# An embedding norm moved to GpSimd, a reordered start of the attention, a state kept in compact form, and one note per gated step

## The chip, the cores and the metric

The program runs on one core of one Trainium2 chip. The metric is the device time of one execution in microseconds. Engines are called by the names of the profile: PE is TensorE (PEld its weight loads), DVE is VectorE, ACT is ScalarE, POOL is GpSimd, SP is the engine whose queue issues the loads.

## The reference

Three stages follow each other; all is float32.

```python
# 1. gated linear attention, B,H,S,D = 4,8,768,40
m_new = np.maximum(f_gate[:, :, t] + m, i_gate[:, :, t])
f_stab = np.exp(f_gate[:, :, t] + m - m_new)
i_stab = np.exp(i_gate[:, :, t] - m_new)
C = f_stab[:, :, None, None] * C + i_stab[:, :, None, None] * np.einsum('bhd,bhe->bhde', vt, kt)
n = f_stab[:, :, None] * n + i_stab[:, :, None] * kt
h_tilde = np.einsum('bhde,bhe->bhd', C, qt)
denom = np.maximum(np.abs(np.einsum('bhd,bhd->bh', n, qt)[:, :, None]), 1.0)
y[:, :, t] = o * h_tilde / denom                      # o = sigmoid(o_gate)
# 2. mixture of 8 experts on the 3072 rows of 320, one expert a row
en = expert_emb / (np.linalg.norm(expert_emb, axis=-1, keepdims=True) + 1e-06)
logits = xn @ en.T / tau                              # xn: rows normed alike
expert_idx = np.argmax(logits, axis=1)
h = np.maximum(x[mask] @ w1[e], 0.0)                  # F = 1024
out[mask] = gate_w[mask, None] * (h @ w2[e])
# 3. gated unit, F = 1536
gate = 1.0 / (1.0 + np.exp(-(x @ w_gate)))
val = x @ w_val
out = (gate * val) @ w_out
```

## The kernel before

**Attention.** The 768 steps are cut into 6 chunks c of 128; with 4 batches b that makes 24 tiles, i = 4c + b. A tile goes through hand-written steps. `st_S` multiplies keys and queries of the 8 heads on PE into two PSUM banks; DVE masks each bank (`am`, and the second in place), ACT casts both to f16 (`ah`), and the remainders `al` are subtracted, the first half on POOL, the second on DVE. `st_V` weights the values on POOL (`vw`), `st_V2` splits them into `vh` (ACT) and `vl` (POOL). `st_AV` multiplies: for c > 0 first the queries with the state `cst[b]` (L464), then the three products of `ah`, `al` with `vh`, `vl` (L471 to L473). `st_U` multiplies keys and weighted values into bank 5 (`u_ps`, L484), and its `add` brings that into the state: for chunk 0 two ACT copies (L493), afterwards two DVE operations (L495). Even heads lie on partitions 0 to 39, odd ones on 64 to 103, hence two of each. `post_ops` divides by the denominator on DVE (`den`, `x0`) and multiplies with the gate on POOL; `st_XT` transposes the result on PE, ACT copies it (`xt`), and `st_logit` multiplies with the transposed, normed embedding `enT`; DVE copies the result to `rs`. `warm(n)` are n matmuls without use.

Each engine runs its instructions in the order in which the code issues them. In the main loop over i, PE's order is the state product and AV of tile i, XT of i-1, U of i, S of i+3, the logits of i-1. Tiles 0 to 3 and the S of tiles 1 to 5 stand ahead of the loop, written out.

**Gates.** `gate_ops` are six DVE operations on 32 rows (two scans, four sums); they run for chunk 0, for chunk 1, and once for chunks 2 to 5 (512 wide). `st_gexp` takes exponentials on ACT, `st_gates2` transposes them on PE (for chunks 2 to 5 into bank 5) and copies them on DVE to `w_all` and `ri_all`. `sideq` is a list of such small operations, and `side(n)` issues n of them wherever it stands. The square root of the embedding norm is a seed and three Newton steps of three operations, on 8 x 1 elements (`sqrt_ops`), on DVE, through `sideq`.

**Experts** follow, then the **gated unit** in 72 steps t. `gated_a(t)` and `gated_b(t)` make gate and value in two PSUM banks out of a ring of four; each bank is written first from one half of the rows and then from the other, and between the two halves PE waits for a tiny ACT copy, `note`, that waits for the first (`turn_rows`). Then follow a sigmoid on ACT, a product on DVE (both `sgm`), a cast on ACT (`hh`), a remainder on POOL (`hl`) and the second product, `gated_l2h(t - 2)`, on PE. Steps 0 and 1 begin together: both `gated_a`, then both `gated_b`. `group_x` splits the input of a later group with an ACT cast (L209) and a POOL subtraction.

Of the kernel before, what the change touches and what calls it, by code (L numbers as in the profile page):

```python
# [22 lines left out]
def kernel(  # L23
# [250 lines left out]
    def kpart(i):  # L274
        return kv[i % NKV][:, KO:VO].rearrange("p (h d) -> p h d", d=D)
# [28 lines left out]
    def emb_norm():  # L304
        esq = ap_.tile([NE, DM], F32, name="esq")
        en1 = ap_.tile([NE, 4], F32, name="en1")
        return [
            lambda: nc.scalar.activation(out=esq, in_=eb, func=AF.Square, accum_out=en1[:, 0:1])
        ] + sqrt_ops(ap_, en1[:, 1:2], en1[:, 0:1]) + [
            lambda: nc.vector.tensor_scalar(  # L310
                out=en1[:, 2:3], in0=en1[:, 1:2], scalar1=1e-6, scalar2=tb, op0=ALU.add, op1=ALU.mult
            ),
            lambda: nc.vector.reciprocal(en1[:, 3:4], en1[:, 2:3]),
            lambda: nc.vector.tensor_scalar_mul(eb, eb, en1[:, 3:4]),
        ]
# [15 lines left out]
    for j in range(4):  # L331
        if j:
            load_qk(j)
        load_kv(j)
        if j == 1:
            nc.sync.dma_start(out=eb, in_=emb)
            nc.sync.dma_start(out=tb, in_=tau.rearrange("(a b) -> a b", a=1).to_broadcast([NE, 1]))
# [55 lines left out]
    def emb_T():  # L393
# [6 lines left out]
        nc.vector.tensor_copy(enT[:, 0:2].rearrange("p a b -> p (a b)"), tp[:, 0:2 * NE])  # L400
        nc.vector.tensor_copy(enT[0:RM, 2], tp[0:RM, 2 * NE:3 * NE])
# [74 lines left out]
    def st_U(i):  # L476
# [92 lines left out]
    def st_rank(c):  # L569
# [14 lines left out]
        pf = bp.tile([P, B, NE], F32, tag="pf", name="pf")  # L584
# [116 lines left out]

    for op in gate_ops(0, L):
        op()
    st_gexp(0, L)
    st_S(0, lambda: st_gates2(0, 1))
# [6 lines left out]
    def early(i):  # L712

        st_AV(i)
        post[i] = post_ops(i)
        weave(post[i][0:3] + post[i][4:5], [side] * 4)


    sideq += gate_ops(L, 2 * L)
    st_V(0)  # L720
    side(6)
    st_V2(0)
    sideq += emb_norm()
    side(1)
    act_zero(qk[0])
    st_gexp(L, 2 * L)
    st_S(1)
    st_V(1)
    st_V(2)
    st_S(2, lambda: (early(0), st_V2(1)))  # L730
# [9 lines left out]
    st_S(3, lambda: early(1))  # L740
    st_U(1)
    st_V2(3)
    side(2)
    post[1][5]()
    load(5)
    st_S(4, lambda: (st_XT(0), early(2), side(len(sideq))))
    st_sig(2)
    load_kv(6)
    post[2][5]()
    st_V(4)  # L750
    st_U(2)
    st_S(5, lambda: (st_XT(1), emb_T(), st_AV(3), st_post(3)))
    sideq += gate_ops(2 * L, S)
    GX = 5
    for i in range(3, NTILE - B):
        load(i + 4)
        if i > 3:
# [3 lines left out]
            st_V2(i + 1)  # L761
            post = post_ops(i)
# [3 lines left out]
        else:  # L766
            warm(5)
# [27 lines left out]
        def between():  # L795
            if add:
                add()
            st_logit(i - 1)

        then = (lambda: st_logit(1)) if i == 3 else first_rows if i == NTILE - B - 1 else None  # L800
        st_S(i + NAHEAD, then, between)
# [8 lines left out]
        if i == GX:  # L810
            st_sig(GX + 1)
            st_gexp(2 * L, S)
# [787 lines left out]
    def gated_a(t):  # L1600
# [6 lines left out]
        note(ins[-1], "l1")  # L1607

    def gated_b(t):
        g, f = order2[t]  # L1610
        fs = slice(f * P, (f + 1) * P)
        for kk in range(2):
# [4 lines left out]
            if kk == 0 and "l1" in passed:  # L1617
# [509 lines left out]
```

## Time and profile before

| | us |
|---|---|
| median of 3 runs (lowest, highest) | 763.08 (761.12, 763.3) |
| profiled execution, its own time | 759.18 |
| its span, first to last instruction | 757.4 |
| PE busy in the span | 727.0 |
| DVE, ACT, POOL busy | 403.3, 364.5, 397.4 |
| mean granted clock of PE, share of full | 0.993 |

The profiled execution is 3.9 us shorter than the median of the timed ones. The 1.8 us between its time and its span lie outside the instructions.

### The profile page before, as it was taken

Reading aid. Unit: us, or ns where it says so; the run is one execution under the profiler, and the core shown is the slowest. Engines: PE = TensorE matmul, PEld = TensorE weight load, DVE = VectorE, ACT = ScalarE, POOL = GpSimd, SP = SyncE. Lnnn points to the kernel's source line nnn. Section 1 sums busy time; section 2 is a strip of 40 time slices with the busy share of each in tenths; the row PEclk is TensorE's granted clock in tenths of the full one; section 3 lists DMA queues with packets and bytes.
Section 4 is the critical chain, followed back from the end, with each engine's and each line's share of the span. In section 5 each row is a group of like instructions: output and inputs, shape, how many; then the busy total and the mean of one; then the engine's idle time right before and its main releaser. Section 6 shows DMA issues by size and latency. Waiting matters only on the chain. (4 is left out here: it accounts for less than half of the span.)

```text
span 757.4 us, 17682 instructions
## 1 busy us (share of the span) xinstructions
PE 727.0 (96%) x6906; PEld 645.3 (85%) x6906; DVE 403.3 (53%) x864; ACT 364.5 (48%) x829; POOL 397.4 (52%) x449
## 2 busy tenths in 40 slices
PE   6889999899999999999899999999999999999995
PEld 5779998799888989999688888888888888888884
DVE  7897999877778777865566664132121111111111
ACT  5765664645965656665454444333333333333322
POOL 6767887757766777886053233542324324324222
PEclk9999999999999999999999999999999999999999
DMA  7654875545455556651112210000000000000001
GB/s 221 193 160 122 265 217 162 168 119 163 146 153 160 157 158 193 185 150 53 53 57 81 81 54 19 37 35 2 1 12 27 2 1 37 1 2 35 2 1 39
DMA packets 39864, 70.46 MB, mean 93 GB/s; under 512 B 4818, under 2 KB 28460, under 8 KB 39772
## 3 DMA queue, kind: packets, MB, share of 16 engines
q1 hardware_dynamic: 36764, 59.61, 26.7%
q0 software_dynamic: 3008, 9.64, 3.9%
q8 instruction: 56, 0.92, 0.5%
q14 instruction: 36, 0.29, 0.1%
HBM read 60.55 MB, written 8.68 MB: 91 GB/s over the span
## 5 line engine op out<-in xcount | busy, mean ns | idle before, releaser
L1634 POOL TENSOR_TENSOR hl<-sgm,hh 128x512 fp32r<-128x512 f32 x71 | 95.1, 1342 | 228.5 <-ACT hh L1633 228.4
L1623 DVE TENSOR_TENSOR sgm<-v_ps,sgm 128x512 f32<-128x512 f32 (+1 forms) x73 | 49.8, 683 | 231.8 <-ACT sgm L1622 231.8
L1659 PE MATMUL o_ps<-wo,hl 64*128 64x320 f32 x560 | 87.2, 307 | 0.0
L1658 PE MATMUL o_ps<-wo,hh 64*128 64x320 f32 x560 | 86.7, 305 | 0.0
L1657 PE MATMUL o_ps<-wo,hh 64*128 64x320 f32 x560 | 86.4, 304 | 0.0
L1622 ACT ACTIVATE sgm<-g_ps 128x512 f32<-128x512 f32 (+1 forms) x73 | 43.2, 593 | 81.7 <-PE g_ps L1581 74.3
L1593 ACT COPY seen<-zeros 1x1 f32<-1x1 f32 x142 | 27.0, 190 | 105.5 <-PE v_ps L1581 57.6
L1633 ACT CAST hh<-sgm 128x512 fp32r<-128x512 f32 (+1 forms) x73 | 44.8, 615 | 48.1 <-DVE sgm L1623 47.7
L1041 ACT ACTIVATE hh<-h_ps 128x256 fp32r<-128x256 f32 (+7 forms) x72 | 35.3, 490 | 55.1 <-PE h_ps L953 50.1
L1579 PE MATMUL v_ps<-xg,wvh 64*128 64x512 f32 x144 | 56.6, 393 | 2.4 <-ACT seen L1593 2.4
L1657 PEld LDWEIGHTS o_ps<-wo,hh 64*128 64x128 f32 x560 | 53.0, 185 | 6.6 <-issue 0.3
L1658 PEld LDWEIGHTS o_ps<-wo,hh 64*128 64x128 f32 x560 | 52.8, 184 | 5.8
L1579 PE MATMUL g_ps<-xg,wgh 64*128 64x512 f32 x144 | 56.6, 393 | 0.0
L1579 PE MATMUL v_ps<-xh,wvh 64*128 64x512 f32 x144 | 56.5, 392 | 0.0
L1579 PE MATMUL g_ps<-xh,wgh 64*128 64x512 f32 x144 | 56.5, 392 | 0.0
L1580 PE MATMUL g_ps<-xg,wgh 64*128 64x512 f32 x144 | 56.4, 392 | 0.0
L1580 PE MATMUL v_ps<-xl,wvh 64*128 64x512 f32 x144 | 56.4, 392 | 0.0
L1580 PE MATMUL v_ps<-xg,wvh 64*128 64x512 f32 x144 | 56.4, 392 | 0.0
L1580 PE MATMUL g_ps<-xl,wgh 64*128 64x512 f32 x144 | 56.4, 392 | 0.0
L1581 PE MATMUL g_ps<-xg,wgl 64*128 64x512 f32 x144 | 56.2, 390 | 0.0
L1581 PE MATMUL v_ps<-xg,wvl 64*128 64x512 f32 x144 | 56.2, 390 | 0.0
L1581 PE MATMUL v_ps<-xh,wvl 64*128 64x512 f32 x144 | 56.2, 390 | 0.0
(354 smaller groups left out, 2603.8 us busy)
## 6 DMA issues: line engine op xcount, KB each, us to landing
kv<-in_kvo_dram SPq DMA_DIRECT2D x24, 484.0 KB
w2raw<-in_moe_w_dram SPq DMA_DIRECT2D x32, 320.0 KB
w1raw<-in_moe_w_dram SPq DMA_DIRECT2D x32, 256.0 KB
qk<-in_qkt_dram SPq DMA_DIRECT2D x48, 160.0 KB
xs<-x SPq DMA_DIRECT2D x24, 192.0 KB
w1raw<-in_moe_w_dram SPq DMA_DIRECT2D x64, 64.0 KB
raw<-in_moe_w_out_dram SPq DMA_DIRECT2D x12, 320.0 KB
raw<-in_moe_w_gate_dram SPq DMA_DIRECT2D x8, 384.0 KB
```

The lines of the kernel that those rows point to most:

```text
L1041: nc.scalar.activation(out=h[f][0], in_=ps, func=AF.Relu)
L1579: lambda: nc.tensor.matmul(ps, at(wh), h[rows, kk], start=start, stop=False),
L1580: lambda: nc.tensor.matmul(ps, at(wh), l[rows, kk], start=False, stop=False),
L1581: lambda: nc.tensor.matmul(ps, at(wl), h[rows, kk], start=False, stop=stop),
L1593: passed[key] = nc.scalar.copy(seen, zeros[0:1, 0:1])
L1622: nc.scalar.activation(out=s[:, cs], in_=pg[:, cs], func=AF.Sigmoid)
L1623: nc.vector.tensor_tensor(out=s[:, cs], in0=pv[:, cs], in1=s[:, cs], op=ALU.mult)
L1633: nc.scalar.copy(gh[:, cs], s[:, cs])
L1634: e.tensor_tensor(out=gl[:, cs], in0=s[:, cs], in1=gh[:, cs], op=ALU.subtract)
L1657: lambda: nc.tensor.matmul(o, gh[rows, ts_], wh[rows], start=begin, stop=False),
L1658: lambda: nc.tensor.matmul(o, gh[rows, ts_], wl[rows], start=False, stop=False),
L1659: lambda: nc.tensor.matmul(o, gl[rows, ts_], wh[rows], start=False, stop=end),
```

## The change

Five things change together. (1) The norm of the embedding: DVE keeps the two operations of the seed and a reciprocal; the three Newton steps and what follows are 11 operations on POOL, right behind the first `st_V`; the scaling of the embedding is one ACT operation; its load stands three loads earlier. (2) In the first tiles `post_ops` and the copies of `st_gates2` come behind the masks instead of ahead of them (argument `last` of `st_S` in the place of `then`), `warm(2)` stands behind AV of tiles 1, 2 and 3, and three of the five behind tile 3 stay; the gates of chunks 2 to 5 begin one to two tiles earlier. (3) `cc[b]`, 128 x 4 x 41, holds the state without the split by heads: from chunk 2 on one DVE operation on 104 partitions adds to it, in chunk 1 two; two ACT copies spread it to `cst[b]`. So that partitions 40 to 63 of the bank hold numbers, the even heads' matmuls in `st_U` take 64 columns of keys instead of 40. POOL clears the four `cc` at the start. (4) `note` has a key for each step t, where before step 1 overwrote that of step 0, which then waited for step 1 while step 1 waited for nothing. (5) An ACT sigmoid on one column stands ahead of step 0, and `group_x` for group 1 moves from the steps 1, 2, 3 to 2, 3, 4.

```diff
+    cc = [bp.tile([P, NPR, DV], F32, name=f"cc{b}", bufs=1) for b in range(B)]
+    for t in cc:
+        nc.gpsimd.memset(t, 0.0)
...
+    def norm_seed():
+        yi = en_y.bitcast(I32)
+        nc.vector.tensor_single_scalar(out=yi, in_=en_sq.bitcast(I32), scalar=1, op=ALU.logical_shift_right)
...
+    def norm_steps():
+        g = nc.gpsimd
+        two = lambda o, x, u, w, op0, op1: g.tensor_scalar(out=o, in0=x, scalar1=u, scalar2=w, op0=op0, op1=op1)
+        for _ in range(3):
+            two(en_t, en_y, en_sq, en_y, ALU.mult, ALU.mult)
+            two(en_t, en_t, -0.5, 1.5, ALU.mult, ALU.add)
+            g.tensor_tensor(out=en_y, in0=en_t, in1=en_y, op=ALU.mult)
+        g.tensor_tensor(out=en_y, in0=en_y, in1=en_sq, op=ALU.mult)
+        two(en_t, en_y, 1e-6, tb, ALU.add, ALU.mult)
+
+    def norm_scale():
+        nc.vector.reciprocal(en_r, en_t)
+        nc.scalar.activation(out=eb, in_=eb, func=AF.Copy, scale=en_r)
...
         for h in range(H):
             u, pr_ = h % 2, h // 2
+            n = D if u else DP
             nc.tensor.matmul(
-                pu[DP * u:DP * u + D, pr_ * DV:(pr_ + 1) * DV], kpart(i)[:, h], vw[:, h], start=True, stop=True
+                pu[DP * u:DP * u + n, pr_ * DV:(pr_ + 1) * DV], kv[i % NKV][:, h * D:h * D + n], vw[:, h],
+                start=True, stop=True,
             )
 
         def add():
-            for u in range(2):
-                sl = slice(DP * u, DP * u + D)
-                pv = pu[sl, 0:NPR * DV].rearrange("p (a d) -> p a d", a=NPR)
-                if c == 0:
-                    nc.scalar.activation(out=cst[b][sl, :, u], in_=pv, func=AF.Copy, scale=SQ)
-                    continue
+            pv = pu[:, 0:NPR * DV].rearrange("p (a d) -> p a d", a=NPR)
+            both = [slice(DP * u, DP * u + D) for u in range(2)]
+            if c == 0:
+                for u, sl in enumerate(both):
+                    nc.scalar.activation(out=cst[b][sl, :, u], in_=pv[sl], func=AF.Copy, scale=SQ)
+                return
+            before = [(sl, cst[b][sl, :, u]) for u, sl in enumerate(both)]
+            if c > 1:
+                before = [(slice(0, DP + D), cc[b][0:DP + D])]
+            for sl, old in before:
                 nc.vector.scalar_tensor_tensor(
-                    out=cst[b][sl, :, u], in0=pv, scalar=SQ, in1=cst[b][sl, :, u], op0=ALU.mult, op1=ALU.add
+                    out=cc[b][sl], in0=pv[sl], scalar=SQ, in1=old, op0=ALU.mult, op1=ALU.add
                 )
+            for u, sl in enumerate(both):
+                nc.scalar.copy(cst[b][sl, :, u], cc[b][sl])
...
-    st_S(0, lambda: st_gates2(0, 1))
+    st_S(0, None, lambda: (st_gates2(0, 1), norm_seed()))
...
-    sideq += gate_ops(L, 2 * L)
     st_V(0)
-    side(6)
+    norm_steps()
+    weave(gate_ops(L, 2 * L))
...
-    st_S(2, lambda: (early(0), st_V2(1)))
+    st_S(2, lambda: (st_AV(0), st_V2(1)), lambda: first_post(0))
...
-    st_S(3, lambda: early(1))
+    st_S(3, lambda: (st_AV(1), warm(2)), lambda: first_post(1))
...
+    sideq += gate_ops(2 * L, S)
+    side(1)
...
-    GX = 5
+    GX = 4
...
-        note(ins[-1], "l1")
+        note(ins[-1], t)
...
-            if kk == 0 and "l1" in passed:
-                turn_rows(ins[0], "l1")
+            if kk == 0:
+                turn_rows(ins[0], t)
...
-    xsteps = {1 + u: (1, u) for u in range(3)}
+    xsteps = {2 + u: (1, u) for u in range(3)}
...
         if t == 0:
+            nc.scalar.activation(out=dum, in_=zeros[:, 0:1], func=AF.Sigmoid)
             gated_a(0)
```

What moves is seen in the order of the instructions. The first place is DVE at tiles 0 and 1 (`sq_y`, `sq_t` and `en` belong to the norm, `den` and `x` to the denominators). Before:

```order
L455 TENSOR_TENSOR al<-s_ps,ah 128x512
L389 TENSOR_SCALAR w_all<-tp_r 128x32
L389 TENSOR_SCALAR ri_all<-tp_r 128x32
L524 TENSOR_TENSOR den<-o_ps,ri_all 128x8
L163 SCALAR_TENSOR_TENSOR sq_y<-sq_t,sq_y 8x1
L527 SCALAR_TENSOR_TENSOR den<-o_ps,den 128x8
L161 TENSOR_TENSOR sq_t<-sq_y,en_258 8x1
L530 RECIPROCAL den<-den 128x8
L162 SCALAR_TENSOR_TENSOR sq_t<-sq_t,sq_y 8x1
L532 TENSOR_TENSOR x_414<-o_ps,den 128x320
L163 SCALAR_TENSOR_TENSOR sq_y<-sq_t,sq_y 8x1
L447 TENSOR_TENSOR am<-s_ps,cmask 128x512
```

Now the same tile has its masks first, and no operation of the norm:

```order
L403 TENSOR_SCALAR w_all<-tp_r 128x32
L403 TENSOR_SCALAR ri_all<-tp_r 128x32
L463 TENSOR_TENSOR am<-s_ps,cmask 128x512
L465 TENSOR_TENSOR s_ps<-s_ps,cmask 128x512
L548 TENSOR_TENSOR den<-o_ps,ri_all 128x8
L551 SCALAR_TENSOR_TENSOR den<-o_ps,den 128x8
L554 RECIPROCAL den<-den 128x8
L556 TENSOR_TENSOR x_442<-o_ps,den 128x320
L471 TENSOR_TENSOR al<-s_ps,ah 128x512
```

The norm's steps stand on POOL now, between the weighted values of tile 0 and their remainder `vl`, which stood next to each other before:

```order
L425 TENSOR_TENSOR vw<-kv_128,w_all 128x328
L318 TENSOR_SCALAR en_158<-en_158 8x1 x2
L322 TENSOR_TENSOR en_158<-en_158 8x1
L318 TENSOR_SCALAR en_158<-en_158 8x1 x2
L322 TENSOR_TENSOR en_158<-en_158 8x1
L318 TENSOR_SCALAR en_158<-en_158 8x1 x2
L322 TENSOR_TENSOR en_158<-en_158 8x1
L323 TENSOR_TENSOR en_158<-en_158 8x1
L318 TENSOR_SCALAR en_158<-en_158,tb 8x1
L435 TENSOR_TENSOR vl<-vw,vh 128x328
```

The second place is DVE around the masks of tiles 5 and 6, where the 512 wide operations of the gates (`mt`, `ft`, `Gt`) and the copies of the logits (`rs`) lie. Before:

```order
L455 TENSOR_TENSOR al<-s_ps,ah 128x512
L559 COPY rs<-l_ps 128x8
L359 SCALAR_TENSOR_TENSOR mt<-ft,mt,it 32x512
L363 TENSOR_TENSOR ft<-ft,mt 32x512
L559 COPY rs<-l_ps 128x8
L447 TENSOR_TENSOR am<-s_ps,cmask 128x512
```

Now one of the wide operations stands ahead of the first copy, and the gates are further on:

```order
L471 TENSOR_TENSOR al<-s_ps,ah 128x512
L371 TENSOR_TENSOR ft<-ft,mt 32x512
L583 COPY rs<-l_ps 128x8
L379 SCALAR_TENSOR_TENSOR Gt<-ft,Gt,lim 32x512
L371 TENSOR_TENSOR it<-it,mt 32x512
L463 TENSOR_TENSOR am<-s_ps,cmask 128x512
```

The third place is ACT at steps 0 to 2 of the gated unit (`seen` is a note, `wo` a cast of the last weights). Before:

```order
L1593 COPY seen<-zeros 1x1 x2
L1112 ACTIVATE fa<-fa,relu_b 128x320
L1095 CAST wo<-fb 128x320
L1622 ACT_TABLE_LOAD
L1622 ACTIVATE sgm<-g_ps 128x512
L1633 CAST hh<-sgm 128x512
L1112 ACTIVATE fa<-fa,relu_b 128x320
L1622 ACTIVATE sgm<-g_ps 128x512
L1095 CAST wo<-fb 128x320
L1633 CAST hh<-sgm 128x512
L209 CAST xh<-yT 128x512
L1593 COPY seen<-zeros 1x1 x2
```

Now the table load stands ahead of the notes, and the cast for group 1 is no longer ahead of step 2's notes:

```order
L1752 ACT_TABLE_LOAD
L1752 ACTIVATE dum<-zeros 128x1
L1624 COPY seen<-zeros 1x1 x2
L1143 ACTIVATE fa<-fa,relu_b 128x320
L1126 CAST wo<-fb 128x320
L1653 ACTIVATE sgm<-g_ps 128x512
L1664 CAST hh<-sgm 128x512
L1143 ACTIVATE fa<-fa,relu_b 128x320
L1653 ACTIVATE sgm<-g_ps 128x512
L1126 CAST wo<-fb 128x320
L1664 CAST hh<-sgm 128x512
L1624 COPY seen<-zeros 1x1 x2
```

## Rows read from the trace of the kernel before

**Rows 1.** Windows: busy by engine (PE, PEld, DVE, ACT, POOL), granted clock, DMA.

```profile
16.00:31.00 15.00, 11.50 (x141) 10.35 (x139) 12.47 (x39) 9.49 (x21) 10.52 (x14) 0.89 0.55 157
...
45.00:62.00 17.00, 13.72 (x184) 11.78 (x184) 13.87 (x41) 9.41 (x21) 10.89 (x17) 0.90 0.56 171
62.00:120.00 58.00, 57.06 (x895) 53.24 (x894) 52.90 (x152) 36.27 (x85) 47.12 (x73) 1.00 0.67 202
```

**Rows 2.** Waits of PE from 0 to 62 us: total us, times, longest.

```profile
PE u_ps L484 <- ACT cst L493: 2.1, 2, 1.2
...
PE tp_x L543 <- DVE rs L559: 1.4, 1, 1.4
```

**Rows 3.** Windows, columns as in rows 1: the first stretch at half clock.

```profile
26.70:30.10 3.40, 3.40 (x30) 3.32 (x25) 3.34 (x12) 1.53 (x5) 1.86 (x3) 0.50 0.50 139
```

**Rows 4.** Timeline of PE: start us, us, line, operation, count.

```profile
14.81 0.18 PE L471 MATMUL o_ps<-vh,ah 128*128 128x41 f16 x1
...
21.30 2.05 PE L435 MATMUL s_ps<-qk 128*128 128x128 f32 x16
...
27.06 3.48 PE L435 MATMUL s_ps<-qk 128*128 128x128 f32 x16
...
31.67 1.24 PE L426 MATMUL warm_ps<-ones_bf 128*128 128x512 bf16 x5
...
42.09 0.73 PE L555 MATMUL l_ps<-enT,xt 128*128 128x8 f32 x6
42.68 1.10 PE L464 MATMUL o_ps<-cst,qk 128*128 128x82 f32 x8
...
44.85 0.63 PE L543 MATMUL tp_x<-ident,x 128*128 128x128 f32 x3
...
57.40 2.00 PE L464 MATMUL o_ps<-cst,qk 128*128 128x82 f32 x8
...
60.85 0.49 PE L543 MATMUL tp_x<-ident,x 128*128 128x128 f32 x3
```

**Rows 5.** Timeline of DVE, columns as in rows 4.

```profile
21.40 0.79 DVE L161 TENSOR_TENSOR sq_t<-sq_y,en 8x1 f32<-8x1 f32 x1
...
36.90 1.11 DVE L363 TENSOR_TENSOR ft<-ft,mt 32x512 f32<-32x512 f32 x1
...
54.81 0.69 DVE L447 TENSOR_TENSOR am<-s_ps,cmask 128x512 f32<-128x512 f32 x1
...
56.02 0.66 DVE L495 SCALAR_TENSOR_TENSOR cst<-u_ps,cst 40x164 f32<-40x164 f32 x2
```

**Rows 6.** Timeline of POOL, columns as in rows 4.

```profile
12.58 0.81 POOL L419 TENSOR_TENSOR vl<-vw,vh 128x328 f16<-128x328 f32 x1 [0.57 <-ACT vh L418]
...
52.95 1.04 POOL L583 TENSOR_TENSOR run<-run,sel 128x8 bf16<-128x8 bf16 x4
```

**Rows 7.** Groups by form: count, busy us, mean ns; L493 from 0, others from 62, to 120 us.

```profile
L493 ACT ACTIVATE cst<-u_ps 40x164 f32<-40x164 f32 x8 | 2.4, 302 | 0.0
...
L464 PEld LDWEIGHTS o_ps<-cst,qk 128*128 128x128 f32 x96 | 11.7, 192 | 0.0
...
L495 DVE SCALAR_TENSOR_TENSOR cst<-u_ps,cst 40x164 f32<-40x164 f32 x24 | 7.7, 320 | 0.2
...
L484 PEld LDWEIGHTS u_ps<-vw,kv 128*40 128x40 f32 x192 | 4.7, 118 | 2.5 <-PE tp_x L543 2.4
```

**Rows 8.** Timelines of ACT and PE at steps 0 to 2 of the gated unit.

```profile
371.18 1.28 ACT L1622 ACT_TABLE_LOAD   x1
...
378.35 0.61 ACT L209 CAST xh<-yT 128x512 fp32r<-128x512 f32 x1
378.87 0.41 ACT L1593 COPY seen<-zeros 1x1 f32<-1x1 f32 x2
...
379.11 0.50 PE L1579 MATMUL v_ps<-xg,wvh 64*128 64x512 f32 x1 [2.01 <-ACT seen L1593]
```

**Rows 9.** Waits of PE from 100 to 160 us, columns as in rows 2.

```profile
PE s_ps L435 <- DVE am L447: 0.8, 1, 0.8
```

More of the change, by code (lines that the diff above doesn't have):

```diff
@@ L302 @@
     nc.scalar.activation(out=dum, in_=zero, func=AF.Exp)
[L304 to L315, printed above, removed]
+    esq = ap_.tile([NE, DM], F32, name="esq")
+    en1 = ap_.tile([NE, 4], F32, name="en1")
+    en_sq, en_y, en_t, en_r = (en1[:, j:j + 1] for j in range(4))
+    def norm_seed():
+        yi = en_y.bitcast(I32)
+        nc.vector.tensor_single_scalar(out=yi, in_=en_sq.bitcast(I32), scalar=1, op=ALU.logical_shift_right)
+        nc.vector.tensor_scalar(
+            out=yi, in0=yi, scalar1=-1.0, scalar2=float(0x5F3759DF), op0=ALU.mult, op1=ALU.add
+        )
+    def norm_steps():
[10 more added lines that the diff above has]
+        nc.scalar.activation(out=eb, in_=eb, func=AF.Copy, scale=en_r)
     nc.gpsimd.memset(qk[1], 0.0)
@@ L333 @@
             load_qk(j)
+        if j == 0:
+            nc.sync.dma_start(out=eb, in_=emb)
         load_kv(j)
         if j == 1:
-            nc.sync.dma_start(out=eb, in_=emb)
             nc.sync.dma_start(out=tb, in_=tau.rearrange("(a b) -> a b", a=1).to_broadcast([NE, 1]))
@@ L700, in side @@
                 sideq.pop(0)()
+    nc.scalar.activation(out=esq, in_=eb, func=AF.Square, accum_out=en_sq)
     for op in gate_ops(0, L):
@@ L710, with first_post @@
     post = {}
-    def early(i):
-        st_AV(i)
+    def first_post(i):
         post[i] = post_ops(i)
-        weave(post[i][0:3] + post[i][4:5], [side] * 4)
-    sideq += gate_ops(L, 2 * L)
+        weave(post[i][0:3] + post[i][4:5])
     st_V(0)
-    side(6)
+    norm_steps()
+    weave(gate_ops(L, 2 * L))
     st_V2(0)
-    sideq += emb_norm()
-    side(1)
     act_zero(qk[0])
     st_gexp(L, 2 * L)
-    st_S(1)
+    st_S(1, None, norm_scale)
     st_V(1)
     st_V(2)
-    st_S(2, lambda: (early(0), st_V2(1)))
+    st_S(2, lambda: (st_AV(0), st_V2(1)), lambda: first_post(0))
     load(4)
@@ L739 @@
     post[0][5]()
-    st_S(3, lambda: early(1))
+    st_S(3, lambda: (st_AV(1), warm(2)), lambda: first_post(1))
     st_U(1)
     st_V2(3)
-    side(2)
     post[1][5]()
     load(5)
-    st_S(4, lambda: (st_XT(0), early(2), side(len(sideq))))
+    sideq += gate_ops(2 * L, S)
+    side(1)
+    turned = []
+    st_S(
+        4, lambda: (turned.extend(emb_T()), st_XT(0), st_AV(2), warm(2)),
+        lambda: (weave(turned), first_post(2)),
+    )
     st_sig(2)
@@ L749 @@
     post[2][5]()
+    side(1)
     st_V(4)
     st_U(2)
-    st_S(5, lambda: (st_XT(1), emb_T(), st_AV(3), st_post(3)))
-    sideq += gate_ops(2 * L, S)
-    GX = 5
+    st_S(5, lambda: (st_XT(1), st_AV(3), warm(2)), lambda: st_post(3))
+    side(1)
+    GX = 4
     for i in range(3, NTILE - B):
@@ L797, in between @@
                 add()
+            if i == 3:
+                st_logit(1)
             st_logit(i - 1)
-        then = (lambda: st_logit(1)) if i == 3 else first_rows if i == NTILE - B - 1 else None
-        st_S(i + NAHEAD, then, between)
+        st_S(i + NAHEAD, first_rows if i == NTILE - B - 1 else None, between)
         if i > B and i % B == 1:
```

15 lines of the change are left out of this document (8 added, 7 removed).

## The prediction

> **What bounds the kernel now.** I began with PE's busy time by stretches, because a faster DVE, ACT or POOL pays only where PE stands still for it. From 62 to 120 us PE is busy 57.06 of 58.00 us at the full clock [rows 1]: a tile there costs what PE needs, and time freed on DVE (52.90) or ACT (36.27) buys nothing. Two stretches ahead of it are different. PE is idle for 3.50 us of 16 to 31 and for 3.28 us of 45 to 62, and their mean granted clock is 0.89 and 0.90 [rows 1]. Together 6.8 us idle.
>
> The view of PE's waits names the releasers: 2.1 us for ACT to empty the bank of `u_ps` into the state, 1.4 us for a DVE copy of logits [rows 2]. Both queue behind something else. ACT's copies stand behind its casts, which wait for DVE's masks, and the masks stand behind the norm's operations on 8 numbers, one of which took 0.79 us [rows 5]. So the reader should see a queue, not a slow instruction.
>
> After each of the two idle stretches PE runs at half clock, 1.2 instead of 2.4 GHz, for about 3.4 us; the first is granted 0.50 over 3.40 us [rows 3]. The price is read from equal work. S with 16 matmuls took 3.48 us there and 2.05 us at the full clock: 1.4 us. From the start of the state product to the transposes it was 60.85 - 57.40 = 3.45 us in the second and 44.85 - 42.68 = 2.17 us otherwise: 1.3 us [rows 4]. What the first tiles lose is therefore 6.8 + 2.7 = 9.5 us.
>
> Much later, at step 2 of the gated unit, PE waits 2.01 us for a note [rows 8].
>
> **The change, part by part.** The sum is made on the profiled execution of 759.18 us, which is 3.9 us under the median of the runs; I carry the difference over to the median, 763.08.
>
> *First tiles.* With the norm off DVE and the masks ahead of the denominators, the chain mask, cast, state copy runs earlier, and the waits of 16 to 62 us lose their cause; nothing in the rows gives a reason for the half clock to come back without them. That is a gain of up to 9.5 us. Four things are paid out of it.
>
> Four matmuls without use are new: five took 1.24 us [rows 4], so 1.0 us. They fill waits, but I count them, since I have already counted the waits as gone.
>
> A new wait stands at tile 5's logits. DVE's copy of tile 0's logits, which frees the bank that PE takes next, now stands behind a 512 wide gate operation; such a one took 1.11 us [rows 5]. PE, behind it, holds the logits and state product of the next tile. Between 0 and 1.1 us, I take 1.0, because DVE is the late one of the two here.
>
> A second one: the transposes of the gates of chunks 2 to 5 need bank 5, which the state add of the tile before still reads, and now come directly after S. The masks begin at 54.81 and the adds end at 56.02 + 0.66 = 56.68 [rows 5], 1.9 us; only the logits' matmuls of 0.73 us [rows 4] cover that. I take 1.1 us, between 0 and 1.9.
>
> On POOL the norm's 11 steps stand between `vw` and `vl` of tile 0. Four dependent operations on 8 columns took 1.04 us [rows 6], so 11 take 2.9 us. POOL was free from 12.58 - 0.57 = 12.0 us on [rows 6]; `vl` would then end at 12.0 + 2.9 + 0.8 = 15.7 us, where AV of tile 0 began at 14.81 [rows 4]: 0.9 us late at most, less as far as tile 0's masks, now ahead of the copies of the gates, start POOL earlier. I take 0.4. No row shows such a step beside DVE's gate operations. The nearest is the reverse, DVE's operation of 8 numbers that took 0.79 us [rows 5]; at that length eleven would take 8.7 us and AV would be 6.7 us late. The Trainium skill, SBUF — State Buffer, section "SBUF: two separate sides", says that DVE and GpSimd hold their shared ports for a whole instruction, and that a DVE operation with two SBUF inputs is enough to block the other. By that rule steps on POOL are held as that row was, and the sum would be short of up to 6.3 us more; the trace shows the blocking on DVE's side only.
>
> The first tiles then give 9.5 - 1.0 - 1.0 - 1.1 - 0.4 = 6.0 us.
>
> *State.* ACT gets two copies of 0.30 us [rows 7] in each of the 16 tiles 4 to 19, 9.7 us in all. I cost them at nothing: in the 12 tiles of 62 to 120 us ACT is idle for 21.7 us [rows 1], 1.8 us a tile, and the state they write is needed four tiles on. DVE loses one of two adds of 0.32 us [rows 7] in 12 tiles, 3.8 us, and gains in PE's time only where PE waits for DVE's masks, 0.8 us once near the end of the attention [rows 9]; I take 0.4, between 0 and 0.8. The four clears on POOL are half the size of an operation of 0.81 us [rows 6], so up to 1.6 us; I cost them at nothing, as the loads at the start are the cover, and keep that bound.
>
> The matmuls of `st_U` load 64 columns in place of 40 for four heads. A load of 40 took 118 ns, one of 128 took 192 ns [rows 7]: 0.84 ns a column, 20 ns for 24. Each head is two instructions, so 8 loads a tile, 0.16 us. Where PE is the bound, in 16 tiles, that is 2.6 us; in all 20 tiles 3.2 us, and nothing if the loads lie behind matmuls. I take 2.6: the loads follow one another through the whole of `st_U`, which has little else to hide them. Against it the Trainium skill, TensorEngine Tiling (Array Packing), section "Key Properties", says that different tiles of the array load weights and multiply in parallel; even and odd heads are different tiles, and by that rule a longer load could lie beside the other half's matmuls, with a sum of 0 for this term. No row here has 64 columns.
>
> *Gated unit.* The table load of 1.28 us no longer stands ahead of step 0's sigmoid [rows 8], and everything down to step 2's note follows it: the product, the cast, the remainder. The cast for group 1 starts 378.87 - 378.35 = 0.52 us ahead of the note [rows 8] and moves behind it. The note comes 1.8 us earlier, out of a wait of 2.01 us. Between 0.5 (the cast alone) and 2.0; I take 1.8. What group 1 needs of its cast comes four steps later.
>
> Sum: 6.0 + 0.4 - 2.6 + 1.8 = 5.6 us. The profiled execution would take 759.2 - 5.6 = 753.6 us, the median **757.5 us**.
>
> **The rivals.**
> *POOL's steps hold AV of tile 0.* At half way between 0.26 and 0.79 us, 0.53 us each, they take 5.8 us; `vl` ends at 18.6 us and AV is 3.8 us late, 3.4 more than taken: 760.9 us. For it is the row of 0.79 us; against it, that DVE has only six gate operations there, so that not every step can meet one. It decides the verdict from 3.3 us on.
>
> *The loads of `st_U` are hidden.* Then 2.6 us come back: 754.9 us. For it speaks that even and odd heads alternate; against it that PE's loads are busy 53.24 of 58.00 us [rows 1]. This is what the rule on tiles would make of it.
>
> *Slower: ACT's copies stand on the path.* They lie between the casts and the copy `xt` for which PE's logits wait. If all 9.7 us were exposed the time would be 757.5 + 9.7 = 767.2 us. It takes over 5.6 of the 9.7 us, 58%, to turn the sign; ACT's 1.8 us of idle time a tile speak against it.
>
> *The change does not do what it says at the gated unit.* A note per step alone shortens nothing that step 2 waits for, since its note was its own already. If the table load was hidden before and only the cast counts, 1.3 us of the gain go: 758.8 us.
>
> **How the numbers follow.** Chances: my sum 0.45, with a range of its own of 755.5 to 759.5 (one of its new waits more or less); POOL's steps 0.20; hidden loads 0.20; the gated unit without its gain 0.08; slower 0.07. A measurement of this kernel can tell some 0.3%, 2.3 us, from no change, so faster begins under 760.8 us. Faster: all of the sum, of the hidden loads and of the gated case, and half of POOL's case, 0.83; the same 0.11; slower 0.06. For the range, the early end is the hidden loads with both new waits gone as well, 754.9 - 2.1 = 752.8; the late end is POOL's case, 760.9, and a little of its upper bound: 752.8 to 761.3.
>
> **What would show it.** No half-clock stretch once AV of tile 0 has begun; the transposes that stood at 60.85 us [rows 4] about 6 us earlier; a wait of about 1 us ahead of tile 0's or 1's logits, and one of about as much ahead of the transposes of the gates of chunks 2 to 5; AV of tile 0 within half a microsecond of 14.8; `st_U` longer by 0.16 us a tile, and tiles in the steady stretch longer by as much; step 2's wait for its note cut to a fraction. I would be wrong if a half-clock stretch came back (1.3 to 1.4 us each), if DVE's wide gate operations held more than these two waits, or if the steady tiles grew by more than `st_U` does, which would be ACT.

## The result, and the profile after

The changed kernel takes 753.6 us, the median of 4 runs (752.28 to 755.48); the kernel before took 762.1 us in the runs beside it. The ratio is 0.989 (95% interval 0.986 to 0.991): 8.5 us faster, inside the range, and 2.9 us more than the sum of 5.6 us; 753.6 us lies outside the sum's own range of 755.5 to 759.5. The profiled execution took 752.99 us, 6.2 us under that of before. The two totals for the profiled executions are close, but the stages below show that this is in part luck; the other 2.3 us of the gain lie in what the first profile did not show. Two executions among the later runs, 1197.85 us of no_gated and 4005.5 us of the kernel before, belong to a slow state and stand in no median below.

The windows of the changed kernel, columns as in rows 1, the last one a stretch that before ran at the full clock:

```profile
16.00:31.00 15.00, 14.61 (x220) 12.40 (x219) 12.24 (x31) 11.12 (x27) 14.02 (x18) 1.00 0.59 187
45.00:62.00 17.00, 15.79 (x237) 14.36 (x237) 13.20 (x38) 12.79 (x28) 11.79 (x19) 1.00 0.54 175
62.00:120.00 58.00, 57.56 (x867) 53.67 (x864) 49.59 (x143) 40.99 (x104) 46.44 (x74) 1.00 0.65 202
142.90:149.70 6.80, 6.80 (x36) 6.71 (x37) 5.38 (x16) 0.41 (x2) 3.06 (x6) 0.50 0.55 152
```

PE was idle for 6.8 us in the first two [rows 1]; now it is idle for 0.39 and 1.21 us, at the full clock. From 62 to 120 us DVE is busy 3.3 us less and ACT 4.7 us more, and PE is a little fuller than before (57.56 us, 57.06 before). A half-clock stretch has appeared at the end of the attention.

PE's waits from 0 to 62 us (total us, times, longest), to be held against rows 2:

```profile
PE s_ps L451 <- DMA qk<-in_qkt_dram: 4.2, 2, 3.7
PE tp_r L401 <- ACT it L392: 2.1, 1, 2.1
PE tp_r L401 <- DVE cc L517: 1.2, 1, 1.2
PE o_ps L488 <- POOL vl L435: 1.0, 1, 1.0
PE tp_x L567 <- DVE rs L583: 0.2, 1, 0.2
```

The waits of `st_U` for ACT are gone, and that of the transposes for `rs` fell from 1.4 to 0.2 us. The third row is the gates of chunks 2 to 5, which before waited 0.4 us:

```profile
PE tp_r L387 <- DVE cst L495: 0.4, 1, 0.4
```

The fourth row is new at tile 0; the prediction had named both. Behind the fourth stand the norm's steps. POOL's timeline at tile 0 (start us, us, line, operation, count):

```profile
10.64 0.74 POOL L425 TENSOR_TENSOR vw<-kv,w_all 128x328 f32<-128x328 f32 x1
11.36 0.71 POOL L318 TENSOR_SCALAR en<-en 8x1 f32<-8x1 f32 x2
...
12.45 0.93 POOL L318 TENSOR_SCALAR en<-en 8x1 f32<-8x1 f32 x2
...
14.98 0.26 POOL L318 TENSOR_SCALAR en<-en,tb 8x1 f32<-8x1 f32 x1
15.31 0.80 POOL L435 TENSOR_TENSOR vl<-vw,vh 128x328 f16<-128x328 f32 x1
```

Eleven steps from 11.36 to 15.24 us are 3.9 us, 0.35 each. AV of tile 0 began at 14.96 and stood still for `vl` until 16.17:

```profile
16.17 0.18 PE L488 MATMUL o_ps<-vl,ah 128*128 128x41 f16 x1 [1.02 <-POOL vl L435]
```

This wait is not a constant of the kernel. In the eight profiles with the steps on POOL ahead of `vl` it is 0 (early_only, no_warm, best4) or 0.6 to 1.4 us.

The state's groups from 62 to 120 us by form, to be held against rows 7:

```profile
L521 ACT COPY cst<-cc 40x164 f32<-40x164 f32 x22 | 7.2, 328 | 0.1
...
L501 PEld LDWEIGHTS u_ps<-vw,kv 128*64 128x64 f32 x88 | 5.9, 137 | 1.7 <-PE tp_x L567 1.5
...
L501 PEld LDWEIGHTS u_ps<-vw,kv 128*40 128x40 f32 x88 | 4.5, 116 | 0.0
...
L517 DVE SCALAR_TENSOR_TENSOR cc<-u_ps,cc 104x164 f32<-104x164 f32 x11 | 3.5, 316 | 0.0
```

A load of 64 columns takes 21 ns more than one of 40, as predicted (20), and an add on 104 partitions costs what one on 40 did. Whether the longer loads reach PE's time is seen in a whole `st_U`, here in the changed kernel and, in the second fence, in the kernel of the experiment no_state, which has 40 columns:

```profile
61.00 0.66 PE L501 MATMUL u_ps<-vw,kv 128*64 128x41 f32 x16
```

```profile
60.17 0.51 PE L499 MATMUL u_ps<-vw,kv 128*40 128x41 f32 x16
```

They do: 0.15 us a tile.

Step 2 of the gated unit still waits for its note, 1.5 us where the kernel before waited 2.01 [rows 8]:

```profile
373.83 0.50 PE L1610 MATMUL v_ps<-xg,wvh 64*128 64x512 f32 x1 [1.50 <-ACT seen L1624]
```

**The stages of all profiles.** Worked out from each timeline: the time from the start of the first S to that of tile 10, on to that of tile 20, on to the first value product that step 0's note releases, on to the end of the wait at step 2, and on to the end of the last matmul. In brackets the us at the half clock inside. The four marked * ran at a time when the kernel before took 765.7 us (761.3 to 762.1 beside the others), and are compared among themselves.

| kernel | to S of tile 10 | to S of tile 20 | to step 0 | to step 2 | to the end |
|---|---|---|---|---|---|
| before | 58.1 (6.8) | 47.6 | 260.4 | 9.38 | 369.7 |
| before_again * | 59.0 (6.8) | 47.4 | 262.8 (6.8) | 9.37 | 371.7 (3.4) |
| after | 52.8 | 48.2 | 261.2 (6.8) | 7.94 | 368.8 |
| after_again | 54.0 (3.4) | 47.7 | 260.1 (3.4) | 7.94 | 368.8 |
| no_state | 52.1 | 48.0 | 259.2 (3.4) | 7.94 | 368.7 |
| no_gated | 52.1 | 48.4 | 261.0 (3.4) | 9.38 | 370.3 (3.4) |
| early_only | 53.2 (3.4) | 48.0 | 260.9 (3.4) | 9.38 | 370.3 (3.4) |
| u64_before * | 59.5 (9.2) | 48.7 (1.0) | 262.7 | 9.37 | 371.7 (3.4) |
| u40 * | 54.1 (6.8) | 48.4 | 263.0 (3.4) | 7.95 | 370.1 |
| best3 * | 52.4 | 48.0 | 261.7 (3.4) | 7.04 | 370.1 |
| norm_dve | 54.4 (3.4) | 48.0 | 260.5 (3.4) | 7.94 | 368.8 |
| no_warm | 52.2 | 48.0 | 260.7 | 7.95 | 368.8 |
| dum_only | 59.1 (6.3) | 47.7 (0.5) | 261.6 (6.8) | 8.34 | 370.3 (3.4) |
| best4 | 51.0 | 48.2 | 261.1 (6.8) | 7.04 | 368.8 |

Two things in the table belong to the execution and not to the kernel. The attention of no_gated is that of the changed kernel, line by line, and yet it takes 52.1 us up to tile 10 and the changed kernel 52.8, neither with a half-clock stretch. The 0.7 us lie ahead of S of tile 4 (16.86 and 17.57 us after the first S); from there to tile 10 the two take 35.24 and 35.25 us. Between tiles 10 and 20 the same code takes 47.7 to 48.4 us. And the last column holds three delays, at the same three places of the gated unit, in five profiles: 0.3 us each in the first of before, near 571, 637 and 700 us, and 0.4 to 0.5 each in all four marked *, two of which have the new gated unit. Where they come from is open; they are not the change's.

### The profile page after: what moved, and what is told of

Read it like the earlier page. It is cut to its first block, busy times and chain, and to the rows that moved or that the text cites. A ratio compares the mean times of both kernels' runs of the same rounds, so it can differ in the third digit from the quotient of the medians.

```text
span 751.2 us, 17720 instructions
## 1 busy us (share of the span) xinstructions
PE 728.3 (97%) x6910; PEld 650.1 (87%) x6910; DVE 396.0 (53%) x840; ACT 375.5 (50%) x863; POOL 398.4 (53%) x464
```

## The experiments

**The changed kernel again (after_again).** No edit.

> The changed kernel as it is, a second time. In its first profile a half-clock stretch stood at 142.8 to 149.7 us, at the end of the attention, which the kernel before did not have there, and it lost some 2 us of lead. Theory A: it belongs to the chip's state in one execution and not to the order of work; then a second profile is without it or has it elsewhere, and its span is 1.5 to 3 us shorter than 751.2. Theory B: the wait of 1.14 us ahead of the logits there causes it every time; then it stands at 142 to 150 us again and the span is 751 within 0.5. Either way the time is 8 to 9 us under that of the kernel before and the state products take 0.66 us a tile where they took 0.51.

752.62 us, ratio 0.990 (0.988 to 0.993). A half-clock stretch stands at the end of the attention again, but half as long; and a new one stands in the first tiles, behind the wait of 1.2 us at the gates, where the first profile had none. Its window:

```profile
50.30:53.50 3.20, 3.20 (x33) 2.41 (x31) 1.46 (x7) 1.59 (x5) 0.70 (x2) 0.52 0.27 97
```

Neither theory holds as it was put, though the span, 751.1 us, is the one that B named: the same wait of one kernel is followed by the half clock in one execution and not in another. The wait of 1.1 us at the end of the attention is in all fourteen profiles of the table, and 11 have a half-clock stretch behind it. There it costs little: from the logits that waited to the first product of the gated unit the profiles not marked * take 217.6 and 218.3 us without a stretch, 216.8 to 218.1 with one of 3.4 us, and 218.7 to 218.8 with one of 6.8 us. What may take it up is seen in PE's waits: before had two more behind it, from 100 to 160 us,

```profile
PE ix_ps L639 <- DVE oh_b L608: 1.4, 1, 1.4
...
PE r_ps L573 <- DVE sel L567: 0.8, 1, 0.8
```

and the changed kernel has neither.

**One part undone or alone (no_state, no_gated, early_only).** no_state takes the old `st_U` and state, no_gated the old steps of the gated unit, early_only both:

```diff
-            n = D if u else DP
...
-        note(ins[-1], t)
+        note(ins[-1], "l1")
...
-    xsteps = {2 + u: (1, u) for u in range(3)}
+    xsteps = {1 + u: (1, u) for u in range(3)}
...
-            nc.scalar.activation(out=dum, in_=zeros[:, 0:1], func=AF.Sigmoid)
```

> The changed kernel with the state as it was: 40 columns for all heads, two DVE adds into the spread state, no copies by ACT, no compact state. Theory A: the 64 columns cost PE 0.15 us in each of 20 tiles, 3.1 us, and the single add gives back some 0.9 us of short waits between 62 and 120 us; undoing both makes the kernel 1 to 2.5 us faster than the changed one. Theory B: the freed DVE time is what keeps the first tiles without waits; undoing it brings back waits of 1 us or more ahead of 62 us, perhaps a half-clock stretch, and the kernel is 0 to 3 us slower than the changed one.

> The changed kernel with the gated unit as it was (old note, no early table load, the casts for group 1 at steps 1 to 3). Theory A: the steps 0 to 2 gave 1.5 us (the lead over the kernel before grew from 3.8 to 5.35 us there), so that much comes back, and the waits of 0.2 to 0.3 us at steps 0 and 1 return. Theory B: the three later steps at which the lead grew by 0.3 us each belong to this part too; then 2.4 us come back. Theory C: nothing comes back (under 0.5 us), since whatever waits there waits for something that did not move.

> The kernel before with the norm on POOL and the new order of the first tiles alone; state and gated unit as before. Theory A: the first tiles alone make 6 to 6.5 us, and the state products' 40 columns keep them: 6 us under the kernel before, at tile 10 a lead of about 6.2 us, no half-clock stretch ahead of 62 us. Theory B: the order pays only with the single add; then the lead at tile 10 is under 4 us and a half-clock stretch is back. The 11 steps on POOL hold AV of tile 0 by the same 1.0 us as in the changed kernel under both.

All four ran side by side; the kernel before took 761.3 us there.

| kernel | median us | ratio, interval |
|---|---|---|
| after_again | 752.62 | 0.990 (0.988 to 0.993) |
| no_state | 752.27 | 0.990 (0.988 to 0.992) |
| no_gated | 755.56 | 0.993 (0.991 to 0.996) |
| early_only | 756.43 | 0.995 (0.992 to 0.997) |

*The state part* changes the median by 0.4 us. The intervals overlap so far that the medians can't tell this from nothing, nor rule out the 1 us at theory A's lower end; the stages say more. From S of tile 4 to that of tile 10 no_state takes 34.91 us, the changed kernel 35.25: the part costs 0.3 us there (the 0.75 us up to tile 10, 52.82 - 52.07, hold the first four tiles, and no_gated, with the part, takes 52.10). Between tiles 10 and 20 no_state's 47.95 us lies inside what the kernels with the part take. So theory A's 1 to 2.5 us is too much, and B's waits did not come back in the first tiles. What pays for the 0.15 us a tile is seen in PE's waits from 62 to 120 us, here of no_state:

```profile
PE u_ps L499 <- PE tp_x L558: 1.1, 3, 0.5
PE ord_ps L630 <- POOL run L598: 0.3, 1, 0.3
```

The changed kernel has 0.2 us of waits in that stretch, for a load. The view names a transpose on PE for `u_ps`, but the timelines show what ended late: in each of the three waits `st_U` starts 0.10 us after the second of the two adds has ended (64.82 and 64.92 us, 83.96 and 84.06, 103.08 and 103.19). One add frees `st_U`'s bank earlier than two.

*The gated unit* is worth 2.9 us (755.56 - 752.62), beside 4.2 us between early_only and no_state. Theory A's 1.5 us is there (9.38 - 7.94 = 1.44), as much again lies behind it, and 0.5 us ahead of it, where the table counts it in the column to step 0: from the first product of the gated unit to the one that step 0's note releases it is 4.81 us in before and no_gated, 4.31 in the changed kernel. There step 0 waited for step 1's note, which the note per step ends. In before:

```profile
369.73 0.49 PE L1579 MATMUL v_ps<-xg,wvh 64*128 64x512 f32 x1 [0.34 <-ACT seen L1593]
```

no_gated waits at steps 0 to 2 as before does:

```profile
PE v_ps L1610 <- ACT seen L1624: 2.4, 2, 2.0
PE g_ps L1610 <- ACT sgm L1653: 0.3, 1, 0.3
PE v_ps L1610 <- DVE sgm L1654: 0.2, 1, 0.2
```

and the products behind the longer wait run at the half clock (the same stretch in its windows):

```profile
375.00:378.30 3.30, 3.30 (x20) 2.78 (x22) 2.34 (x4) 1.17 (x4) 2.14 (x2) 0.53 0.32 94
```

That costs 370.33 - 368.75 = 1.6 us in the last column. Theory B is wrong: the three later delays of 0.3 us are in neither no_gated nor early_only, and two profiles with the new gated unit, u40 and best3, have them.

*The first tiles* alone give 761.3 - 756.4 = 4.9 us; up to tile 10 they are 4.8 us ahead with a half-clock stretch inside (theory A: 6.2 without), and no_state, the same up to there, 6.0 us without one. The norm did not hold AV of tile 0 at all in early_only's profile, against the expectation.

**The kernel before again (before_again).** No edit.

> The kernel before as it is, a second profile. Its first one took 759.18 us where its runs have a median of 761 to 763. Theory A: the first was a lucky execution at the gated unit: the two kernels run since with the old gated unit both showed a half-clock stretch of 3.4 us behind the wait of 2.01 us at step 2, and it did not. Then this profile has such a stretch near 379 us and takes 760.5 us or more, while the three delays of 0.3 us at 570 to 700 us, which none of the later profiles shows, are gone. Theory B: the difference comes from the first tiles; then there are three half-clock stretches ahead of 150 us and none at step 2.

764.47 us. Two stretches at the half clock that the first profile did not have, at steps 2 and 3 of the gated unit and at the end of the attention; the first tiles have 6.8 us of it in both:

```profile
383.50:386.80 3.30, 3.30 (x22) 2.97 (x21) 3.23 (x6) 1.80 (x4) 1.26 (x2) 0.50 0.34 99
...
148.00:154.70 6.70, 6.62 (x34) 6.55 (x35) 5.21 (x15) 0.57 (x2) 3.21 (x6) 0.50 0.58 167
```

Theory A holds, but for its last clause: the three late delays are here again, 0.5 us each. Of six profiles with the wait of 2.0 us at step 2, five have a half-clock stretch behind it, the first profile of before being the sixth; of the eight with a wait of 1.5 or 0.6 us, none. The clock of the timed runs fits: the 14 of the kernel before beside the last experiments had mean granted clocks of 0.984 to 0.991, the slowest (763.42 us) 0.984 and the quickest (759.88 us) 0.991. The first profile, with 0.993 and 759.18 us, was at the quick end.

**The 64 columns by themselves (u64_before), and ACT's copies (u40).**

```diff
-                pu[DP * u:DP * u + D, pr_ * DV:(pr_ + 1) * DV], kpart(i)[:, h], vw[:, h], start=True, stop=True
+                pu[DP * u:DP * u + (D if u else DP), pr_ * DV:(pr_ + 1) * DV],
+                kv[i % NKV][:, h * D:h * D + (D if u else DP)], vw[:, h], start=True, stop=True
```

```diff
-            n = D if u else DP
+            n = D
...
-                before = [(slice(0, DP + D), cc[b][0:DP + D])]
+                before = [(sl, cc[b][sl]) for sl in both]
```

> The kernel before with one edit: the even heads' matmuls of the state product load 64 columns in place of 40 (the further rows of the bank are written and never read). Theory A: each state product takes 0.15 us more on PE and in the stretch from 62 to 120 us, where PE is the bound, each tile as much; over all 20 tiles 2 to 3 us slower than the kernel before. Theory B: the stretch absorbs it, since DVE's two adds are what PE waits for there by 0.2 to 0.3 us; then under 1 us slower.

> The changed kernel with 40 columns for all heads and therefore two DVE adds a tile into the compact state; ACT still spreads it. Against the changed kernel without its state part (752.3 us) it differs by ACT's 32 copies and by where the adds write. Theory A: ACT's copies lie in its idle time, so it stands within 1 us of that, in the profile too between 62 and 120 us. Theory B: the copies hold ACT's copy of the transposed tile, for which the logits wait, by part of 9.7 us; then it is 2 us or more slower than that.

u64_before: 764.7 us, the kernel before 765.7, ratio 0.9985 (0.997 to 1.000), so not slower, as theory B had it for the whole time. The stage points the other way: between tiles 10 and 20 it took 1.3 us more than before_again, with a half-clock stretch that reaches 1.0 us into it. Nine of its ten runs have a clock of 0.988 to 0.992, the kernel before 0.979 to 0.989, which may have made up for it. Whether that follows from the edit, behind which PE's two short waits for the bank (0.7 us in before_again) are gone, or from chance stays open.

u40: 756.37 us, ratio 0.987 (0.984 to 0.989). Its ten tiles from S of tile 10 take 0.46 us more than those of best3, which differs there by ACT's copies and by where the adds write. Theory A: the copies cost 0.05 us a tile at most, a difference no larger than the 0.7 us by which one kernel's profiles differ in that stage.

**Three waits at once (best3).** The state as before, and

```diff
-    norm_steps()
     weave(gate_ops(L, 2 * L))
     st_V2(0)
+    norm_steps()
...
-        tp = bank(5, "tp_r") if lo > 1 else tp_ps("tp_r")
+        tp = tp_ps("tp_r")
...
-        weave(rest[1])
+        if t != 1:
+            weave(rest[1])
         s = gated_b(t)
+        if t == 1:
+            weave(rest[1])
```

> The changed kernel with four further edits: the state part undone, the norm's steps on POOL behind the remainder of tile 0's values, the transposes of the gates of chunks 2 to 5 into the ring of two banks instead of bank 5, and at step 1 of the gated unit the splitting of the weights behind the product in place of ahead of it. Theory A: the three waits left (1.0 us at AV of tile 0, 1.2 us at the gates, 1.5 us at step 2) go, each without a new one of its size, and the half-clock stretch near 50 us goes with them; 2.5 to 4.5 us under the changed kernel, about 749 us. Theory B: the first wait only moves, since the logits of tiles 0 and 1 then wait for a later norm, and the ring's banks wait for the copies of the logits; then 1.5 us at most remain.

754.02 us, ratio 0.985 (0.983 to 0.987), beside a kernel before that was slower than the one beside the changed kernel; the stages are the better comparison. Only the third edit did what it was made for (7.94 to 7.04 us up to step 2). PE's waits from 0 to 62 us:

```profile
PE tp_r L400 <- DVE rs L574: 1.4, 1, 1.4
PE o_ps L486 <- DVE x L547: 0.8, 2, 0.4
PE s_ps L450 <- DVE al L470: 0.5, 1, 0.5
```

The wait at the gates is as long in the other bank, because that bank waits for a copy that stands in the same DVE queue behind the same masks and adds. The wait at AV of tile 0 came back as two of 0.4 to 0.5 us a little later. For these two theory B holds in that the waits only moved.

**The norm on DVE (norm_dve), no filling (no_warm), the early table load (dum_only).**

```diff
-        g = nc.gpsimd
+        g = nc.vector
```

```diff
-    st_S(3, lambda: (st_AV(1), warm(2)), lambda: first_post(1))
+    st_S(3, lambda: (st_AV(1)), lambda: first_post(1))
```

The second is made for tiles 2 and 3 too; the third adds the sigmoid on one column, and nothing else, to the kernel before.

> The changed kernel with the norm's 11 steps on DVE instead of POOL, at the same place in the code (ahead of the gate operations of chunk 1). Theory A: where the steps stand costs little, since the order of the masks made the gain: the wait of 1.0 us at AV of tile 0 goes, DVE is later by 11 short operations (2 to 3 us), which delay the masks of tiles 1 and 2 by less than that; up to tile 10 within 1 us of the changed kernel. Theory B: the move to POOL made the gain: waits of 1 us and more come back ahead of 30 us with a half-clock stretch, 2 to 4 us more up to tile 10.

> The changed kernel without the six matmuls without use behind AV of tiles 1, 2 and 3 (the three behind tile 3 stay). Theory A: they only fill time that PE would have to wait in or could use, so up to tile 10 the kernel is 0 to 1.2 us earlier and no half-clock stretch comes back ahead of 40 us. Theory B: they keep the clock up: without them waits of 0.5 us or more stand in their place and a half-clock stretch follows near 27 us; then 1 to 2 us later.

> The kernel before with one edit: the sigmoid on one column ahead of step 0 of the gated unit, which loads ACT's table early. Theory A: the load of 1.28 us stood on the path to step 2, so the wait of 2.01 us there falls to 0.7 to 1.0 us, and the half-clock stretch behind it may go too; the three short waits at steps 0 and 1 (0.34, 0.33, 0.23 us), which are PE waiting for a note of the other step, stay. Theory B: DVE's splitting of the weights ahead of step 1's product holds the note; then the wait stays at 1.5 to 2.0 us and the load is worth 0.5 us at most.

norm_dve: 755.21 us, ratio 0.992 (0.989 to 0.994). Up to tile 10 it takes 54.4 us where after_again, with a half-clock stretch at the same place, takes 54.0; the wait at AV of tile 0 is gone. Theory A for that stage: which engine does the norm can't be told from nothing there, since one attention differs by 0.7 us between executions. For the whole time the interval overlaps that of the changed kernel.

no_warm: 754.56 us, ratio 0.990 (0.988 to 0.992). Up to tile 10 it takes 52.2 us, as no_gated does with the six matmuls (52.1), and no half-clock stretch lies between AV of tile 0 and the last matmul. Two waits came instead, 0.7 us at the logits and 0.5 us at AV, of which B had warned, but no half clock behind them. Theory A: these six matmuls buy nothing in this execution. The profiled execution was the quickest of the four (751.73 us, clock 0.996); the others took 754.0 to 755.1 at 0.988 to 0.991, so whether they keep the clock up in other executions stays open.

dum_only: 760.69 us, ratio 0.998 (0.996 to 1.000). The stage shrinks by 1.04 us, but the wait at step 2 stays:

```profile
PE v_ps L1579 <- ACT seen L1593: 2.3, 2, 2.0
```

Theory A is wrong on the wait; B has the wait right and the worth wrong. The note comes 1.04 us earlier, and so does PE. The two short waits for `sgm`, 0.33 and 0.23 us, were the table load's and are gone, and with them the 0.5 us in which a gate product ran without a value product beside it (373.12 to 373.61 us in before). The wait at step 0, 0.35 us, stays: it is the note's. What is left of the wait of 2.0 us is DVE's queue, as best4 shows.

**A better kernel (best4).** The changed kernel with the third edit of best3, and

```diff
-            warm(2 if i < 8 else i > NTILE - B - 4)
+            if i == GX + 2:
+                st_gates2(2, NCH)
+            else:
+                warm(2 if i < 8 else i > NTILE - B - 4)
...
-        if i == GX + 1:
-            st_gates2(2, NCH)
```

> The changed kernel with two edits: at step 1 of the gated unit the splitting of the weights stands behind the product (alone it cut the stage of steps 0 to 2 from 7.94 to 7.04 us), and the transposes of the gates of chunks 2 to 5 stand one tile later, behind AV of tile 6, in the place of the matmuls without use there. Theory A: the wait of 1.2 us at the gates goes, and the half-clock stretch that followed it in two of five executions with it; together 2 to 3.5 us under the changed kernel, and no half-clock stretch ahead of 140 us. Theory B: the state product of tile 6 then waits for DVE's copies of those transposes by as much; then 0.9 to 1.2 us.

750.85 us (750.16 to 751.14), ratio 0.985 (0.983 to 0.987), 1.8 us under after_again with the kernel before at 761.5 beside it; a little under theory A's 2 us. The intervals overlap, but each of its four runs is shorter than each of the ten of the changed kernel (751.6 us and more). The wait at the gates is gone, and up to tile 10 it takes 51.0 us without a half-clock stretch. The other edit is seen on DVE at step 1, first in the changed kernel, then in best4 (`fb` and `fa` split the weights, `sgm` is the product that the note waits for):

```profile
370.19 1.35 DVE L1144 SCALAR_TENSOR_TENSOR fb<-raw,fa 128x320 int32<-128x320 int32 x1 [0.15 <-ACT fa L1143]
371.58 0.33 DVE L1147 TENSOR_SCALAR fa<-fb 128x320 int32<-128x320 int32 x1
371.94 0.49 DVE L1129 SCALAR_TENSOR_TENSOR wo<-fc,fa 128x320 fp32r<-128x320 int32 x1
372.35 0.68 DVE L1654 TENSOR_TENSOR sgm<-v_ps,sgm 128x512 f32<-128x512 f32 x1
```

```profile
368.77 0.69 DVE L1655 TENSOR_TENSOR sgm<-v_ps,sgm 128x512 f32<-128x512 f32 x1 [0.64 <-ACT sgm L1654]
369.38 0.48 DVE L1145 SCALAR_TENSOR_TENSOR fb<-raw,fa 128x320 int32<-128x320 int32 x1
```

The product now comes first. What is left of the wait:

```profile
PE v_ps L1611 <- ACT seen L1625: 0.6, 1, 0.6
```

## Why the prediction was right, and where it was not

**The carry-over to the median failed.** The profile was treated as the kernel's usual execution less a constant of 3.9 us. What the runs show instead are half-clock stretches that most executions of before have and the first profile did not: the one at step 2 stands in five of six profiles and costs 1.6 us. In the eight profiles with the change at that place it is gone, and that is part of why the median fell by more than the profiled execution. An estimate for the 3.9 us: the median clock of the 14 runs above is 0.9865, 0.0065 under the profile's 0.993; over 757 us that is some 10 us more at half clock, 3.5 to 4.6 us at 1.2 to 1.6 us for each 3.4, and less where stretches at the end of the attention are among them. Which stretches the timed runs had, no trace shows.

**That 6.2 us came out near 5.6 is luck in part.** By the table's columns it is 5.3 - 0.6 - 0.8 + 1.4 + 1.0. The 1.0 us are the three delays in the first profile of before, which no part of the change removed; the 0.8 us lost hold a half-clock stretch of 6.8 us in the profile after.

**First tiles: 6.0 us predicted, 5.3 measured** up to tile 10 (58.1 - 52.8), and 6.0 in no_gated's profile of the same attention. The two idle stretches and both half-clock stretches went, as the queue of masks, casts and copies had it. The four payments were each off: the unused matmuls cost nothing that can be told (no_warm against no_gated) where 1.0 us was taken for four more; the logits' wait 0.12 us where 1.0 was taken (the copy of tile 0's logits begins at 33.66 us, when S of the next tile is just done); the gates 1.21 us (1.1); POOL's steps 1.0 us in this profile (0.4), at 0.35 us a step and not 0.26. "No half-clock stretch once AV of tile 0 has begun" was wrong: the changed kernel has one at the end of the attention, and after_again one behind the very wait at the gates that the prediction foresaw without seeing what may follow it.

**State: -2.2 us predicted, -0.3 measured** from tile 4 to tile 10, and nothing beyond the spread in the ten tiles after. The loads were right to 1 ns, and `st_U` grew by 0.15 us (0.16). The term that was mis-sized is DVE's: 0.4 us was taken from the wait for masks near the end of the attention, which did not shrink (0.8 us in both), while the gain came from the waits of `st_U` for its bank, which the add releases. The prediction followed DVE's time to the masks and forgot the bank that the add itself holds. The rival of hidden loads is refuted for the loads, though the time came out near its 754.9 us. The Trainium skill, TensorEngine Tiling (Array Packing), section "Key Properties", says that different tiles can load weights and multiply in parallel; the trace does not show that for this chain of 16 small matmuls, since eight loads of 21 ns more made it 0.15 us longer. The slower rival, ACT's copies on the path, cost at most 0.5 us in ten tiles and not 58% of 9.7.

**Gated unit: 1.8 us predicted, 3.5 measured in no_gated's profile, 2.9 between the medians.** From the first product to the end of step 2's wait it is 14.20 us before and 12.25 after, 1.95 us: 1.04 the table load (1.28 taken), 0.50 the note per step, and 0.40 the rest, the cast's place (0.52 taken). The other 1.6 us are half clock that no row of the first profile showed. The prediction put the note per step at nothing because step 2's note was its own already; it overlooked step 0, which waited 0.34 us for step 1's. "Step 2's wait for its note cut to a fraction" failed: it fell from 2.01 to 1.50 us. The step that failed is that PE was taken to stay where it was: it reaches the wait 1.4 of the 1.95 us earlier too, since the waits at steps 0 and 1 went. The chain then ended at DVE, where a splitting operation took 1.35 us beside POOL's remainder `hl`:

```profile
369.77 1.42 POOL L1665 TENSOR_TENSOR hl<-sgm,hh 128x512 fp32r<-128x512 f32 x1 [13.84 <-ACT hh L1664]
```

best4, where it starts behind that remainder, shows 0.48. The trace of the changed kernel has five such operations that started while POOL ran: each ended 0.35 us after POOL's, whether 0.30 or 1.00 us of that was left. The Trainium skill, SBUF — State Buffer, section "SBUF: two separate sides", says that of a GpSimd operation and a DVE operation with two SBUF inputs whichever starts first has the shared ports for its whole instruction, and the other waits. The trace agrees for DVE; POOL's small steps, 0.35 us each, were hardly held.

**POOL's steps held AV** for 0 to 1.4 us, not the rival's 3.8. In norm_dve, with the steps on DVE, the wait vanishes and no time is gained by tile 10 that one execution could show.

## What to carry to other kernels

Two executions of one program can differ by which waits are followed by a half-clock stretch: before a sum is made, the profile's own mean granted clock is to be held against that of the timed runs, and a wait of 2 us counts for itself and for the stretch that may follow, where no later wait takes that up. A stage is to be compared over several profiles of the same code: here two differed by 0.7 us in the first tiles. A wait names its last releaser; moving the operation to another bank or engine helps only if it leaves the queue that is late (best3 against best4). Here a shorter operation on a shared bank paid at the next writer of that bank, not at what the engine did next. And where several waits follow each other, what comes earlier for one may come earlier for PE too: the gain at the last wait is less than the note's own.

## What the runs showed of the hardware

The half clock is not fixed by the program: the wait of 1.2 to 1.4 us at the gates was followed by it in four profiles of nine, the 2.0 us at step 2 in five of six, 1.5 us there in none of six, and the price is 1.2 to 1.4 us at the gates and 1.6 us at step 2 for a stretch of 3.4 us. At the end of the attention 6.8 us of it cost 0.5 to 1.2 us more than none, where PE has fewer later waits for DVE. A DVE operation with two SBUF inputs that started inside a POOL operation ended 0.35 us after that in each of five cases in the changed kernel, up to 1.35 us long where it takes 0.49 to 0.56 when POOL is not running as it starts. An ACT copy from the compact state of 164 numbers on 40 partitions takes 328 ns, and a DVE add on 104 partitions 316 ns against 320 on 40 [rows 7].
